# q and k of the later batches transposed by the DMA crossbar instead of TensorE, in a fused window-attention and MLP kernel

## Chip, cores and metric

The kernel runs on one core of a Trainium2 chip. The metric is the device time of one execution in microseconds. Before the change it is 324.88 us (median of two runs, 324.31 to 325.46).

## The reference

```python
# q, k, v: (8 batches, 8 heads, 576 tokens, 64), fp32
scores = q @ k.T / sqrt(64); masked to the 64 newest tokens (0 <= i - j < 64)
x = softmax(scores) @ v                      # then heads are joined: (8, 576, 512)
xn = (x - mean) / sqrt(var + 1e-6) * g_ln
out = x + relu(xn @ w_ch1) @ w_ch2           # 512 -> 2048 -> 512, fp32
```

One caution. The inputs are small (0.1 times a normal draw), so the softmax is nearly flat. "Correct" is therefore weak evidence that q and k are laid out right.

## The kernel before

There are nine groups. Group g (0 to 7) runs the MLP of the first 512 tokens of batch g; group 8 runs it for the four "tails" (the last 64 tokens of each batch, two batches in one tail). From group 2 on, a group is 30 units of TensorE work: 16 of the first layer (`l1`), 14 of the second. The attention of later batches is slotted between these units by `at(unit, function, ...)`. Each engine runs its instructions in this program order.

```python
def load_qk(b, half):                        # b >= 2: 4 tokens (1 KB) in one run
    ...
    nc.sync.dma_start(out=t[:, :].rearrange("p (h m) -> p h m", h=4),
        in_=src[b, 4*half:4*half+4, 0:SM, :].rearrange("h (p j) d -> p h (j d)", j=4))

def t_main(b, x, half, eng=None):            # TensorE transposes, then an eviction
    src = qk16.pop((b, x, half))
    tp = t_tile([128, 8, 128], f"tp_{b}_{x}_{half}")
    for i in range(8):
        nc.tensor.transpose(out=tp[:, i, :], in_=src[:, i], identity=ident16)
    ...
    evac(...)                                # ScalarE in the later batches

def t_tail(i, x): ...                        # the same for a tail: 4 (q) or 8 (k) transposes

# the schedule, groups g > 1; b = g + 1, n = g + 2 (cut)
TAILS = {3: [0], 5: [1], 7: [2, 3]}          # group: tails whose attention runs in it
at((2, 7, 12, 17)[j], b_step, b, j)          # values into xps (one PSUM tile), normalise into x_norm
at(1, s_mm, NGRP-1, i)                       # scores of a tail, slot 1 of its group
at(11, cast_qk, n, 0); at(16, cast_qk, n, 1) # GpSimd, fp32 -> fp16
at(17, t_main, n, 0, 0); ...                 # slots 17, 19, 21, 25
at(17, load_qk, n+1, 0); at(18, load_qk, n+1, 1); at(23, load_v, n+1, 0, 4)
at(27, s_mm, n, 0)                           # first scores of batch n
at(24, cast_tail, i); at(27, t_tail, i, 0); at(29, t_tail, i, 1)  # group before the tail's
# units 27 and 29 store two blocks each: nc.sync.dma_start(out=out[...], in_=x_norm...)
```

The loads of q, k, v and the weights and all stores but one at the very end are issued by SyncE and share one in-order queue.

The softmax here doesn't subtract the row's maximum and nothing guards it: scores larger than these inputs give would overflow.

## Time and profile before

| | before |
|---|---|
| time, median | 324.88 us |
| span of the profiled execution | 322.6 us |
| TensorE busy, share of the chain of waits | 96%, 85% |
| mean granted TensorE clock | 0.996 |
| one steady group (2 to 6) | about 33 us |

From the page of the kernel before, the slices: one digit for each fortieth of the span, in tenths; `PEclk` is the granted TensorE clock, `DMA` the mean busy share of the DMA engines. Below it, the chain that ended last, by engine.

```profile
PE   7978999999989999999999999999999999999993
...
PEclk9999999999999999999999999999999999999998
DMA  8999999976089947904598459000570190003013
...
PE 85%; DVE 4%; SPq 3%; DMA 2%; POOL 2%; ACT 1%; issue 0%; ACTq 0%; POOLq 0%
```

The PE row is what bounds the kernel: from the fifth slice on it is nearly always 9. DMA has room on average, but not everywhere.

The chain that ended last, in order of time (start, duration, what), around the end of group 2. These are the transposes that the change removes:

```profile
117.87 0.55 PE tp L216 x8
...
120.39 0.45 PE tp L216 x8
...
131.36 0.45 PE tpk L237 x8
```

Eight transposes lengthen the chain by 0.45 us (the first eight of a group by 0.55). The busy column of the grouped view says more (some 220 ns each), because matmuls overlap.

The same stretch by windows of 2 us (window, length, then busy us and instructions of PE, weight loads, DVE, ACT and POOL, the clock, the DMA share and GB/s):

```profile
116.00:118.00 2.00, 2.00 (x34) 1.62 (x33) 1.97 (x5) 0.38 (x1) 1.80 (x4) 1.00 0.99 347
...
126.00:128.00 2.00, 2.00 (x24) 1.84 (x23) 1.11 (x2) 0.77 (x1) 2.00 (x5) 1.00 0.92 223
...
132.00:134.00 2.00, 2.00 (x25) 0.89 (x23) 0.09 (x1) 1.78 (x3) 0.00 (x0) 1.00 1.28 254
```

At 116 us the DMA engines are full with 1 KB q and k runs, at 347 GB/s; at 126 us they are nearly full with 256-byte v runs, at 223 GB/s; at 132 us they are still full, with stores. (The share, as the profile counts it, can exceed 1.) Two lines of the timeline show who will need the queue's output next (start, duration, engine, line, instruction, and in brackets the idle time before it and what ended it):

```profile
133.47 0.41 PE L263 MATMUL sc<-tqT,tkT 64*128 64x64 f16 x16
...
135.66 0.69 DVE L297 TENSOR_TENSOR xn<-xps,rcp 128x512 f32<-128x512 f32 x1 [0.19 <-DMA out_dram<-xn]
```

A tail's scores start 1.7 us into group 3, and VectorE already waits 0.19 us for the last store of group 2, whose buffer it overwrites.

### The profile page before, as it was taken

The page shows a single profiled execution, that of the slowest core. Times are in us where ns is not written, and L with a number is a line of the kernel's source. Part 1 is how long each engine was busy: PE and PEld are TensorE (multiplying, and loading weights), DVE is VectorE, ACT ScalarE, POOL GpSimd, SP SyncE. Part 2 cuts the span into 40 slices and gives each one's busy share as a digit, 9 for nine tenths or more (in the row PEclk, how much of TensorE's full clock was granted, in tenths as well). Part 3 has the DMA queues.
Part 4 walks back from the last instruction along what each step waited for, and adds up shares of the span by engine and source line. Part 5 has one row for each costly group of instructions (what it writes and reads, how often), then busy time and mean ns, then how long its engine had stood idle before and what let it go on. Part 6 is the DMA issues. An engine that isn't in the chain of part 4 may idle for free.

```text
span 322.6 us, 7813 instructions
## 1 busy us (share of the span) xinstructions
PE 309.6 (96%) x3229; PEld 204.6 (63%) x3229; DVE 204.3 (63%) x388; ACT 176.8 (55%) x292; POOL 164.6 (51%) x251
## 2 busy tenths in 40 slices
PE   7978999999989999999999999999999999999993
PEld 4556444687544578656964696459755865694582
DVE  0887764666885795489447954896559644751643
ACT  2576624487346754876457647775486157405600
POOL 7678765423991689079705982598036506200000
PEclk9999999999999999999999999999999999999998
DMA  8999999976089947904598459000570190003013
GB/s 194 282 385 259 363 306 295 264 267 133 35 276 227 207 139 204 241 2 133 173 259 183 132 168 259 26 2 2 171 182 2 24 241 33 0 2 131 0 36 98
DMA packets 85639, 51.08 MB, mean 158 GB/s; under 512 B 55682, under 2 KB 76674, under 8 KB 85603
## 3 DMA queue, kind: packets, MB, share of 16 engines
q1 hardware_dynamic: 84816, 48.11, 55.6%
q0 software_dynamic: 640, 2.33, 3.1%
q8 instruction: 25, 0.41, 0.5%
q10 hardware_dynamic: 146, 0.13, 0.1%
q14 instruction: 12, 0.09, 0.1%
HBM read 38.80 MB, written 9.44 MB: 150 GB/s over the span
## 4 chain that ended last, share of the span: by engine, by line
PE 85%; DVE 4%; SPq 3%; DMA 2%; POOL 2%; ACT 1%; issue 0%; ACTq 0%; POOLq 0%
PE hps L363 33%; PE pA L435 11%; PE pC L435 8%; PE pB L435 8%; PE hph L484 6%; PE ch L375 4%; PE xps L291 4%; PE tp L216 3%; PE sc L263 3%; DMA w1s<-in_moe_w_ch_dram 2%; PE ztp L328 2%; SPq L139 2%; POOL w1g L188 1%; PE ch L499 1%; DVE wT L532 1%; SPq L87 1%
## 5 line engine op out<-in xcount | busy, mean ns | idle before, releaser
L363 PE MATMUL hps<-zT,w1g 128*128 128x512 f16 x480 | 112.0, 379 | 0.0
L367 ACT ACTIVATE hrT<-hps 128x512 f16<-128x512 f32 x120 | 71.9, 599 | 35.1 <-PE hps L363 31.6
L363 PEld LDWEIGHTS <-w1g 128*128 128x128 f16 x480 | 44.1, 98 | 47.0 <-issue 1.0
L316 POOL TENSOR_SCALAR rsz<-mvg 128x1 f32<-128x1 f32 x28 | 12.2, 437 | 76.5 <-DVE mvg L302 75.5
L266 ACT ACTIVATE pt<-sc 128x512 f16<-128x512 f32 x72 | 39.0, 595 | 14.6 <-PE sc L263 13.1
L435 PEld LDWEIGHTS <-sS 128*128 128x128 f16 x448 | 43.0, 98 | 4.7
L207 ACT COPY qkT<-tp 128x1024 f16<-128x1024 f16 x26 | 26.2, 1012 | 33.6 <-PE tp L216 32.4
L126 POOL CAST qk<-qk 128x1024 f16<-128x1024 f32 x32 | 33.7, 1070 | 9.5 <-DMA qk<-in_q_dram 4.9
L442 DVE TENSOR_TENSOR xn<-pA,xn 128x512 f32<-128x512 f32 x28 | 19.2, 686 | 26.1 <-PE pA L435 17.4
L331 ACT COPY zT<-ztp 128x512 f16<-128x512 f16 x36 | 21.1, 586 | 26.5 <-PE ztp L328 26.1
L435 PEld LDWEIGHTS <-hrT 128*128 128x128 f16 x336 | 32.3, 98 | 5.0
L294 DVE RECIPROCAL rcp<-xps 128x8 f32<-128x8 f32 x36 | 7.4, 205 | 34.3 <-PE xps L291 34.1
L414 DVE TENSOR_TENSOR sS<-hrT 128x512 f16<-128x512 f16 (+1 forms) x42 | 21.4, 510 | 10.2 <-ACT hrT L367 10.2
L297 DVE TENSOR_TENSOR xn<-xps,rcp 128x512 f32<-128x512 f32 x36 | 24.9, 692 | 3.3 <-DMA out_dram<-xn 2.2
L435 PE MATMUL pA<-wT,sS 128*128 128x256 f16 x224 | 26.9, 273 | 0.0
L435 PE MATMUL pC<-w2s,sS 128*128 128x256 f16 x224 | 26.8, 273 | 0.0
L273 DVE TENSOR_TENSOR pt<-pt,mask 128x1024 f16<-128x1024 f16 x28 | 21.2, 762 | 8.6 <-ACT pt L266 8.5
L484 PE MATMUL hph<-zT,w1g 128*128 128x256 f16 x192 | 23.6, 273 | 2.5 <-ACT zT L331 1.1
L299 DVE BATCH_NORM_STATS2 stats<-xn 128x6 f32<-128x512 f32 x36 | 25.0, 695 | 1.2
L319 POOL TENSOR_SCALAR z<-xn,rsz 128x512 f16<-128x512 f32 x28 | 23.4, 836 | 2.9
L375 PE MATMUL ch<-w2s,hrT 128*128 128x512 f16 x96 | 23.7, 380 | 0.1
L484 PEld LDWEIGHTS <-w1g 128*128 128x128 f16 x192 | 18.0, 98 | 5.8 <-issue 2.2
(85 smaller groups left out, 437.2 us busy)
## 6 DMA issues: line engine op xcount, KB each, us to landing
out_dram<-xn SPq DMA_DIRECT2D x34, 256.0 KB, 3.6
qk<-in_q_dram SPq DMA_DIRECT2D x16, 512.0 KB, 4.8
qk<-in_k_dram SPq DMA_DIRECT2D x16, 512.0 KB, 5.9
v<-in_v_dram SPq DMA_DIRECT2D x32, 256.0 KB, 6.2
w2s<-in_moe_w_ch_dram SPq DMA_DIRECT2D x12, 512.0 KB, 5.6
w1s<-in_moe_w_ch_dram SPq DMA_DIRECT2D x4, 512.0 KB, 7.3
tk<-in_k_dram SPq DMA_DIRECT2D x8, 256.0 KB, 4.4
tv<-in_v_dram SPq DMA_DIRECT2D x8, 256.0 KB, 5.1
```

The lines of the kernel that those rows point to most:

```text
L126: nc.gpsimd.tensor_copy(out=dst[:, :].rearrange("p (a j) e d -> p a e j d", j=j), in_=t[:, :].rearrange("p (a e j d) -> p a e j d", e=2, j ...
L207: nc.scalar.copy(out=out, in_=in_)
L266: nc.scalar.activation(out=pt[:, par], in_=sc[par], func=AF.Exp, bias=0.0, scale=scale)
L297: nc.vector.tensor_tensor(out=xn, in0=xps[:, :, 0:D], in1=rcp_b, op=ALU.mult)
L299: nc.vector.bn_stats(out=stats, in_=xv)
L319: nc.gpsimd.tensor_scalar(out=z, in0=xv, scalar1=rs, scalar2=nm, op0=ALU.mult, op1=ALU.add)
L363: nc.tensor.matmul(out=hps, lhsT=w1g[:, kc, 128 * hc:128 * (hc + 1)], rhs=zT[g][:, kc, :], start=(kc == 0), stop=(kc == NKC - 1),)
L367: nc.scalar.activation(out=hrT[:, hc, :], in_=hps, func=AF.Relu, bias=0.0, scale=1.0)
L375: nc.tensor.matmul(out=ch[kb], lhsT=hrT[:, hc, 128 * kb:128 * (kb + 1)], rhs=w2s[:, hc, :], start=(hc == 0), stop=(hc == NHC - 1),)
L414: nc.vector.tensor_tensor(out=o, in0=x, in1=y, op=op)
L435: nc.tensor.matmul(out=bank[which][:, p, :], lhsT=a[:, c, 128 * p:128 * p + 128], rhs=wv[:, c, :], start=(first and p == 0 and c == 0), st ...
L484: nc.tensor.matmul(out=hps[:, e], lhsT=w1g[:, kc, 128 * hc:128 * (hc + 1)], rhs=zT[g][:, kc, 256 * half:256 * half + 256], start=(kc == 0) ...
```

## The change

The intent: take 176 transposes off the engine that bounds the kernel. q and k of batches 4 to 7 are loaded with a token on each partition, cast into one fp16 tile per tensor, and transposed by the DMA crossbar, one instruction for q and one for k of a batch; the tails likewise.

```diff
+    XQ = 4
+    cast16 = [p_const.tile([128, NHP, 4, 128], FP16, ...) for x in range(2)]
 def load_qk(b, half):
+            elif b >= XQ:
+                for c in range(2):
+                    s0 = 256 * half + 128 * c
+                    nc.sync.dma_start(out=t[:, 512*c:512*c+512]...,
+                        in_=src[b, :, s0:s0 + 128, :].rearrange("h s d -> s h d"))
 def t_main(b, x, half, eng=None):
+        if b >= XQ:
+            if half == 0:
+                dst = flat(b, x)[:, 64 * x:64 * x + NHP * SM]
+                nc.sync.dma_start_transpose(out=dst.rearrange("p (a t) -> p a t", t=128),
+                                            in_=cast16[x][...].rearrange("p a c m -> p (a c m)"))
+            return
 def t_tail(i, x):
+            if XQ < B:
+                nc.sync.dma_start_transpose(out=tailT[i][x]..., in_=src...)
+                return
 # schedule
-            for ... in zip((17, 19, 21, 25), ((0, 0), (1, 0), (0, 1), (1, 1))):
+            for ... in zip((17, 17, 17, 17) if n >= XQ else (17, 19, 21, 25), ...):
                 at(i, t_main, n, x, half, 0)
```

(Cut: the casts into `cast16`, the score matmuls' addressing of the flat layout, fewer zero fills, and a switch `XZ = 99` that leaves another use of the crossbar off.) A k tail is cast into `cast16[1]` too. No load or store moved in the program, but two transposes now stand ahead of the next batch's loads in SyncE's queue.

More of the change, by code (lines that the diff above doesn't have):

```diff
@@ L41 @@
     EPS = 1e-6
+    XQ = 4
+    XZ = 99
     scale = 1.0 / (D ** 0.5)
@@ L77 @@
     qk32, qk16, v32 = {}, {}, {}
+    cast16 = [p_const.tile([128, NHP, 4, 128], FP16, tag=f"cast16_{x}", name=f"cast16_{x}") for x in range(2)]
     tail32, tail16, tailT, vT = {}, {}, {}, {}
@@ L90, in load_qk @@
                 )
+            elif b >= XQ:
+                for c in range(2):
+                    s0 = 256 * half + 128 * c
+                    nc.sync.dma_start(
+                        out=t[:, 512 * c:512 * c + 512].rearrange("p (h d) -> p h d", h=H),
+                        in_=src[b, :, s0:s0 + 128, :].rearrange("h s d -> s h d"),
+                    )
             else:
@@ L110, in cast_tail @@
         q16 = p_in.tile([128, H, D], FP16, tag="tq16", name=f"tq16_{i}", bufs=1)
-        k16 = p_in.tile([128, 2, H, D], FP16, tag="qk16_1", name=f"tk16_{i}")
+        k16 = cast16[1][:, 0:2].rearrange("p r c (e d) -> p r (c e) d", d=D)
         vt = p_va.tile([128, 2, H, D + 1], FP16, tag="vt", name=f"vt_{i}", bufs=1)
@@ L122, in cast_qk @@
             t = qk32.pop((b, x, half))
-            dst = p_in.tile([128, 8, 2, D], FP16, tag=f"qk16_{x}", name=f"qk16_{x}_{b}_{half}")
+            if b >= XQ:
+                nc.gpsimd.tensor_copy(
+                    out=cast16[x][:, :, 2 * half:2 * half + 2, :].rearrange("p a c m -> p c a m"),
+                    in_=t[:, :].rearrange("p (c a m) -> p c a m", c=2, a=NHP),
+                )
+                continue
+            dst = cast16[x][:, 2 * half:2 * half + 2, :, :].rearrange("p a c (e d) -> p (a c) e d", d=D)
             qk16[(b, x, half)] = dst
@@ L202, in alloc_qkT, with flat @@
         qkT[b] = [p_qkt.tile([128, NHP, SM + 64 * x], FP16, tag=f"qkT{x}", name=f"qkT{x}_{b}") for x in range(2)]
-        nc.gpsimd.memset(qkT[b][1][:, :, 0:64], 0.0)
+        if b < XQ:
+            nc.gpsimd.memset(qkT[b][1][:, :, 0:64], 0.0)
+        else:
+            nc.gpsimd.memset(qkT[b][1][:, 0, 0:64], 0.0)
+    def flat(b, x):
+        return qkT[b][x][:, :, :].rearrange("p h m -> p (h m)")
     def evac(x, out, in_):
@@ L211, in t_main @@
     def t_main(b, x, half, eng=None):
+        if b >= XQ:
+            if half == 0:
+                dst = flat(b, x)[:, 64 * x:64 * x + NHP * SM]
+                nc.sync.dma_start_transpose(out=dst.rearrange("p (a t) -> p a t", t=128),
+                                            in_=cast16[x][:, :, :, :].rearrange("p a c m -> p (a c m)"))
+            return
         src = qk16.pop((b, x, half))
@@ L229, in t_tail @@
                         p_qkt.tile([128, 2, NHP, 128], FP16, tag="tkT", name=f"tkT_{i}", bufs=1))
+            if XQ < B:
+                nc.sync.dma_start_transpose(out=tailT[i][0], in_=src[:, :, :].rearrange("p h d -> p (h d)"))
+                return
             tp = t_tile([128, NHP, 128], f"tpq_{i}")
@@ L233, in t_tail @@
         else:
+            if XQ < B:
+                nc.sync.dma_start_transpose(out=tailT[i][1][:, :, :, :].rearrange("p r h t -> p (r h) t"),
+                                            in_=src[:, :, :, :].rearrange("p r h d -> p (r h d)"))
+                return
             tp = t_tile([128, 2, NHP, 128], f"tpk_{i}")
@@ L258, in s_mm @@
                         rhs = tailT[j][0][rows, hp, 64 * iw:64 * iw + 64]
+                    elif g >= XQ:
+                        c0 = SM * hp + 64 * (2 * j + iw)
+                        lhsT = flat(g, 1)[rows, c0:c0 + 128]
+                        rhs = flat(g, 0)[rows, c0:c0 + 64]
                     else:
@@ L325, in zt_step @@
             zT[g] = p_grp.tile([128, NKC, 512], FP16, tag="zT" + sfx, name=f"zT_{g}", bufs=1 if sfx else 2)
+        if g >= XZ:
+            nc.sync.dma_start_transpose(out=zT[g][:, :, 128 * kb:128 * kb + 128], in_=z)
+            return
         ztp = t_tile([128, NKC, 128], f"ztp_{g}_{kb}")
@@ L745 @@
             at(21, make_vB, n)
-            for i, (x, half) in zip((17, 19, 21, 25), ((0, 0), (1, 0), (0, 1), (1, 1))):
+            for i, (x, half) in zip((17, 17, 17, 17) if n >= XQ else (17, 19, 21, 25),
+                                    ((0, 0), (1, 0), (0, 1), (1, 1))):
                 at(i, t_main, n, x, half, 0)
```

## The prediction

> **What bounds it now.** TensorE. The page's busy table has PE at 96% of the 322.6 us span and the chain of waits gives it 85%; in the steady groups (33 us each, from 99 us) the timeline shows it back to back at full clock. The DMA engines, by stretches of 2 us, are at 0.9 to 1.28 from 126 to 136 us, the end of group 2, when v loads, vB copies and 1 MB of stores overlap; the same in group 4. Their last stores land so late that VectorE's normalise at 135.66 already waits for one (0.19 us; 1.67 us at 170).
>
> **What goes.** Sixteen 8-transpose blocks of batches 4 to 7 (0.45 us of the chain each), four k-tail blocks (0.45) and four q-tail blocks (about 0.22): 7.2 + 1.8 + 0.9 = 9.9 us of TensorE, all on the critical path. ScalarE loses 20 evacuations of 1012 ns and 4 of 588, off the path.
>
> **What comes.** All on SyncE's one in-order queue:
> - q and k loads of these batches in 256-byte runs instead of 1 KB. The old ones ran at 347 GB/s (share 0.99), 256-byte v loads at 223 GB/s (share 0.92). So 2 MB per batch takes about 8.7 us instead of 6.
> - Transposes of 4 + 1.5 MB in all. The Trainium skill, "DMA: Bandwidth & Descriptors", section "Latency and other measured facts", states 261 GB/s for a DMA transpose; no run here shows it yet. Estimate from it: 2 us per 512 KB.
> - Order. The q/k transposes wait for both casts (about 119 to 120 us in group 2), and the next batch's q/k loads (at 114 us before) stand behind them. Then come v, two stores, the q-tail transpose, two stores, and last the k-tail transpose.
>
> **Where it bites (estimates).** From 119 us the queue has 4 us of transposes, 8.7 of q/k, about 10 of v, copies and stores, and 1.5 of tail transposes: the k-tail tile lands near 145 us. The tail's score matmuls want it in slot 1 of the next group (at 133.5 us before, about 131 after the savings), in TensorE's order. So:
> - groups 3 and 5 (tail, after a group with loads): about 14 us of stall each;
> - group 4: its first normalise waits for late stores, and TensorE for the xps bank: about 6 us;
> - group 7: tail, no q/k loads before it: about 4.5 us;
> - first scores of batches 4 to 7: about 1.5 us in all.
>
> Sum: 324.9 - 9.9 + 28 + 6 + 4.5 + 1.5 = 355 us, less a little overlap.
>
> **Predicted: 352 us, 8 in 10 between 327 and 380.** Faster by over 2%: 0.07. Within 2%: 0.07. Slower by over 2%: 0.86.
>
> **What would show each step right.** No TensorE transposes of tq, tk and batches 4 to 7; ScalarE down 22 us. In the list of waits a new, long wait of TensorE for the tail score operands (tkT, released by a DMA), two of more than 8 us; a DVE wait for out_dram of several us at group 4's start. DMA share near 1 from about 120 us to 145 us. Main transposes landing 2 to 6 us after issue. First scores of batches 4 to 7 waiting over 2 us each would mean slower transposes.
>
> **What would make it wrong.** Transposes and loads overlapping better than a shared DMA budget allows: then most of the 10 us remains as a gain (315 to 318). Transposes far slower than 261 GB/s, for instance limited by SyncE issuing many small pieces: each k-tail wait grows by over 10 us, towards 380 and beyond.

## The result, and the profile after

| | before | after |
|---|---|---|
| time, median | 324.88 us | 375.37 us (375.18 to 375.55, 2 runs) |
| ratio of the fast runs | | 1.155 (1.146 to 1.165) |
| span of the profiled execution | 322.6 us | 373.5 us |
| share of the chain: PE, SyncE's queue, DMA | 85%, 3%, 2% | 49%, 19%, 13% |
| mean granted clock | 0.996 | 0.919 |

Ratios are the mean time of one kernel's fast runs over that of the other's fast runs of the same rounds, so they differ a little from the ratio of the medians.

The kernel became 50.5 us slower. The same rows of the page, after:

```profile
PE   7889999999899911999908990099999985999994
...
PEclk9999999999999975899965996579999996999998
DMA  8999999654996999008996299900785094203013
...
PE 49%; SPq 19%; DMA 13%; DVE 7%; POOL 6%; issue 3%; ACT 0%; POOLq 0%; DVEq 0%; ACTq 0%
```

Two things are new in these rows: holes in PE (1, 1; 0; 0, 0; and a shallow one, 8, 5, in group 7), and a 5 to 8 in the clock row at and behind each hole. Before, the clock row was 9 but for the last slice.

The new waits of TensorE, and the one of VectorE behind one of them, from the list of who waited for whom (total us, times, longest):

```profile
PE sc L302 <- DMA tkT<-cast: 40.7, 4, 17.4
...
DVE xn L336 <- DMA out_dram<-xn: 12.1, 1, 12.1
...
PE xps L330 <- DVE pt L312: 9.8, 1, 9.8
...
PE sc L302 <- DMA qkT<-cast: 0.6, 1, 0.6
```

They are six places, which the timeline of TensorE alone shows with the idle time ahead of each in brackets:

```profile
127.93 0.41 PE L302 MATMUL sc<-qkT,qkT 64*128 64x64 f16 x16 [0.59 <-DMA qkT<-cast]
...
148.21 0.61 PE L302 MATMUL sc<-tqT,tkT 64*128 64x64 f16 x16 [16.30 <-DMA tkT<-cast]
...
197.47 0.26 PE L330 MATMUL xps<-vB,pt 128*64 128x65 f16 x1 [9.83 <-DVE pt L312]
...
242.12 0.61 PE L302 MATMUL sc<-tqT,tkT 64*128 64x64 f16 x16 [17.37 <-DMA tkT<-cast]
...
312.43 0.61 PE L302 MATMUL sc<-tqT,tkT 64*128 64x64 f16 x16 [6.18 <-DMA tkT<-cast]
...
323.92 0.41 PE L302 MATMUL sc<-tqT,tkT 64*128 64x64 f16 x16 [0.89 <-DMA tkT<-cast]
```

(The first line is the only wait for a transposed main tile, 0.59 us; then come the tail in group 3, the `xps` bank in group 4, the tail in group 5 and the two tails in group 7.) The main transposes themselves are in time. What is late is the k tail, and SyncE's queue shows why. This is its timeline from the main transposes of group 2 to the k tail's:

```profile
119.21 4.56 SPq L237 DMA_TRANSPOSE qkT<-cast  x2
123.81 1.77 SPq L97 DMA_DIRECT2D qk<-in_q_dram  x2
125.63 3.21 SPq L97 DMA_DIRECT2D qk<-in_k_dram  x2
128.88 4.57 SPq L97 DMA_DIRECT2D qk<-in_q_dram  x2
133.50 1.87 SPq L97 DMA_DIRECT2D qk<-in_k_dram  x2
135.47 4.99 SPq L155 DMA_DIRECT2D v<-in_v_dram  x4
140.55 1.55 SPq L443 DMA_DIRECT2D out_dram<-xn  x2
142.20 1.37 SPq L259 DMA_TRANSPOSE tqT<-tq  x1
143.66 1.00 SPq L443 DMA_DIRECT2D out_dram<-xn  x2
144.75 1.28 SPq L266 DMA_TRANSPOSE tkT<-cast  x1
```

The same queue before, where the q and k loads of batch 5 went out one by one from 114.06 us on, and v and the stores were issued by 133.4 us:

```profile
114.06 0.37 SPq L92 DMA_DIRECT2D qk<-in_q_dram  x1
...
125.07 4.44 SPq L139 DMA_DIRECT2D v<-in_v_dram  x4
129.70 3.70 SPq L401 DMA_DIRECT2D out_dram<-xn  x4
```

After, these loads are issued from 123.81 us. They take 11.6 us to issue, v takes 5.0, and the k tail's transpose leaves at 144.75 us and lands (its data are complete) 3.4 us later. Its score matmuls were ready at 131.9 us. The windows of this stretch:

```profile
121.00:123.00 2.00, 2.00 (x20) 1.80 (x19) 1.67 (x4) 0.00 (x0) 1.76 (x5) 1.00 1.13 200
...
134.00:136.00 2.00, 0.00 (x0) 0.00 (x0) 0.00 (x0) 0.00 (x0) 0.00 (x0) 0.85 0.91 206
...
140.00:142.00 2.00, 0.00 (x0) 0.00 (x0) 0.00 (x0) 0.00 (x0) 0.00 (x0) 0.50 1.15 210
...
150.00:152.00 2.00, 2.00 (x35) 1.10 (x34) 0.69 (x2) 0.80 (x2) 0.00 (x0) 0.50 0.00 0
...
152.00:154.00 2.00, 2.00 (x9) 0.83 (x8) 1.93 (x5) 1.49 (x4) 0.67 (x2) 0.88 0.01 4
```

The DMA engines are busy nearly throughout (a mean share of 0.79 from 132.0 to 135.4 us and of 1.15 from there to 140.5) while the compute engines stand still. And the clock: it is halved from about 135.4 us (0.85 in the window from 134: 1.4 us at full speed, 0.6 at half), 3.5 us after TensorE fell idle, and it stays at half until about 152.5 us, over 4 us after work was back at 148.21. In the other three long stalls it fell 2.4, 2.8 and 3.2 us after TensorE fell idle.

Group 4 has no tail. There the late stores block VectorE, whose normalise overwrites `x_norm`, and TensorE finds `xps` full:

```profile
195.20 0.69 DVE L336 TENSOR_TENSOR xn<-xps,rcp 128x512 f32<-128x512 f32 x1 [12.08 <-DMA out_dram<-xn]
```

### The profile page after: what moved, and what is told of

Its sections match the earlier page's. It is cut to its first block, busy times and chain, and to the rows that moved or that the text cites. A ratio compares the mean times of both kernels' runs of the same rounds, so it can differ in the third digit from the quotient of the medians.

```text
span 373.5 us, 7489 instructions
## 1 busy us (share of the span) xinstructions
PE 309.2 (83%) x3053; PEld 197.8 (53%) x3053; DVE 200.4 (54%) x388; ACT 156.2 (42%) x268; POOL 162.9 (44%) x251
## 4 chain that ended last, share of the span: by engine, by line
PE 49%; SPq 19%; DMA 13%; DVE 7%; POOL 6%; issue 3%; ACT 0%; POOLq 0%; DVEq 0%; ACTq 0%
PE hps L405 22%; SPq L97 9%; PE pA L477 6%; SPq L155 5%; PE hph L526 4%; PE pB L477 4%; PE pC L477 4%; DMA tkT<-cast 4%; DMA w2s<-in_moe_w_ch_dram 3%; DMA qk<-in_k_dram 3%; PE xps L330 3%; PE ch L417 2%; PE sc L302 2%; SPq L443 2%; DMA w1s<-in_moe_w_ch_dram 2%
## 5 line engine op out<-in xcount | busy, mean ns | idle before, releaser
L405 PE MATMUL hps<-zT,w1g 128*128 128x512 f16 x480 | 118.7, 397 | 0.0
L405 PEld LDWEIGHTS <-w1g 128*128 128x128 f16 x480 | 45.9, 101 | 52.0 <-issue 8.5
L302 PE MATMUL sc<-tqT,tkT 64*128 64x64 f16 x64 | 2.2, 226 | 40.7 <-DMA tkT<-cast 40.7
L312 DVE TENSOR_TENSOR pt<-pt,mask 128x1024 f16<-128x1024 f16 x28 | 20.5, 737 | 13.5 <-ACT pt L305 13.4
L330 PEld LDWEIGHTS <-pt 128*64 128x64 f16 x576 | 12.7, 114 | 24.1 <-DVE pt L312 10.8
L302 PEld LDWEIGHTS <-tkT 64*128 64x128 f16 x64 | 1.6, 116 | 42.7 <-DMA tkT<-cast 42.7
```

The lines of the kernel that those rows point to most:

```text
L330: nc.tensor.matmul(out=xps[64 * r:64 * r + 64, h, :D + 1], lhsT=pt[:, par, hp, r, :], rhs=rhs, start=True, stop=True)
L405: nc.tensor.matmul(out=hps, lhsT=w1g[:, kc, 128 * hc:128 * (hc + 1)], rhs=zT[g][:, kc, :], start=(kc == 0), stop=(kc == NKC - 1),)
```

## The experiments

The theories, by the letters of the expectations. **Q**, mine: queue order; the tail transposes and the stores stand behind the next q, k and v loads, in a queue that the main transposes hold up. **X**: the crossbar transposes are too slow in themselves or disturb what runs beside them. **L**: the 256-byte load runs cost the time. For the clock, **I**: TensorE's idle time lowers it; **T**: something else does (power, the crossbar). All twelve kernels gave a result that passed the comparison. "Before" in each comparison is the kernel before (324.5 to 325.2 us median).

| run | what | median us | ratio to before | mean clock |
|---|---|---|---|---|
| e1_tails_pe | tails back on TensorE | 357.28 | 1.098 | 0.954 |
| e3_layout_only | new loads and layout, no crossbar | 327.90 | 1.009 | 0.999 |
| e4_long_runs | crossbar, old 1 KB runs (scrambled) | 365.18 | 1.125 | 0.935 |
| e7_fill | dummy matmuls in the idle stretches | 372.39 | 1.146 | 0.978 |
| e7b_fill_more | the same, enough of them | 373.27 | 1.150 | 1.000 |
| e5_loads_last | next loads last in the queue | 341.68 | 1.052 | 0.971 |
| e10_tails_dma_only | only the tails on the crossbar | 347.56 | 1.070 | 0.973 |
| e8_reordered | queue by deadlines | 332.61 | 1.025 | 0.987 |
| e11_tails_late | e8, tails in groups 6 and 7 | 340.29 | 1.045 | 0.974 |
| b1_before_tails_late | control: before, tails in 6 and 7 | 328.05 (3 fast runs) | 1.010 | 0.996 to 0.998 (its profile is of the slow run) |
| e12_reorder_tails_pe | reordered, tails on TensorE | 318.15 | 0.978 | 0.998 |
| e13_deadline_order | all on the crossbar, reordered further | 321.64 | 0.990 | 0.998 |

### Tails back on TensorE

```diff
 def t_tail(i, x):
-            if XQ < B:        # both branches
+            if False:
```

> The changed kernel with the tails transposed by TensorE again (batches 4 to 7 stay on the crossbar). Theory Q (queue order: the tail transposes stand behind the next batch's loads): the 40.7 us of waits for tkT vanish, but the stores stay late behind the same loads, so groups 3 and 5 now show the wait for xps that only group 4 shows (9.8 us each, hidden until now by the longer tail wait), with a low clock after it. About 375 - 40.7 + 2.7 (transposes back) + 2 x 9.8, less some clock: 350 to 358 us. Theory X (the crossbar itself is slow and hurts all it touches): the time falls only by the tail's own transposes, a few us, to about 368.

Measured: 357.28 us, within Q's range. The waits for `tkT` are gone, and the other wait that the late stores make came to light in all three groups that follow a group with loads. TensorE's timeline:

```profile
149.05 0.65 PE L330 MATMUL xps<-vt,pt 128*64 128x65 f16 x16 [10.46 <-POOL rsz L355]
...
194.09 0.26 PE L330 MATMUL xps<-vB,pt 128*64 128x65 f16 x1 [9.60 <-DVE pt L312]
...
237.09 0.65 PE L330 MATMUL xps<-vt,pt 128*64 128x65 f16 x16 [10.37 <-POOL rsz L355]
```

(The engine named in the brackets is the last of several that the profile saw; the bank `xps` is freed by VectorE.) So the tail transposes alone are not the cause: without them the same queue stops TensorE for 10 us, a few units later in the same groups. X, which expected about 368 us, does not fit.

### Loads and layout alone

Main transposes and tails on TensorE, from the token-by-partition tile; loads and casts as changed.

```diff
 def t_main(b, x, half, eng=None):         # b >= XQ
-            nc.sync.dma_start_transpose(...)
+            tp = t_tile([128, NHP, 2, 128], ...)
+            for hp in range(NHP):
+                for c in range(2):
+                    nc.tensor.transpose(out=tp[:, hp, c, :], in_=cast16[x][:, hp, 2*half + c, :], ...)
+            evac(..., qkT[b][x][:, :, c0:c0 + 256]..., tp)
 def t_tail(i, x):
-            if XQ < B:
+            if False:
-            for ... in zip((17, 17, 17, 17) if n >= XQ else (17, 19, 21, 25), ...):
+            for ... in zip((17, 19, 21, 25), ...):
```

> The new token-by-partition loads, casts and layout for batches 4 to 7, but every transpose on TensorE and no DMA transpose at all. Theory Q: the loads are not held behind transposes and take only about 2.7 us more DMA time per batch; stores land some 3 us later, which TensorE's slack covers: 325 to 330 us. Rival L (the 256-byte runs are what slows it): most of the 50 us stays, 350 us or more.

Measured: 327.90 us, 0.9% slower than before (0.7 to 1.1%). Twice TensorE waits 1.5 us for the k tail's cast, whose buffer is now shared with the main tile. L falls: the short runs by themselves cost under 4 us.

### Crossbar with the old runs

```diff
 def load_qk(b, half):
-            elif b >= XQ:
+            elif False:       # 1 KB runs; the tokens come out scrambled
```

> The changed kernel with batches 4 to 7 read in the old 1 KB runs, wrong result on purpose (tokens end up scrambled), all else the same. Theory Q: each chain from the main transposes to the tail transposes is 2.7 us shorter (8.7 to 6 us of loads), so three stalls shrink by 2 to 4 us each: 364 to 369 us. Rival L: most of the stalls go, below 345 us.

Measured: 365.18 us. The three tail waits are 12.82, 14.63 and 6.09 us instead of 16.30, 17.37 and 6.18, and the wait in group 4 is 3.31 us instead of 9.83, with one more of 2.28 us there for a copy of v (`vB`). So each chain of q and k loads is some 3 us longer through the short runs, which with the layout-only run means: run length matters only where the queue is already late. That this scrambled kernel passed is the caution given with the reference.

### Order alone

```diff
             if n + 1 < B:
-                at(17, load_qk, n + 1, 0)
-                at(18, load_qk, n + 1, 1)
-                at(23, load_v, n + 1, 0, 4)
+                at(30, load_qk, n + 1, 0)
+                at(30, load_qk, n + 1, 1)
+                at(30, load_v, n + 1, 0, 4)
```

> Order alone: the changed kernel with the next batch's q, k and v loads issued at the end of the group, behind the tail transposes and stores, instead of between the main transposes and the stores. Same work, same bytes. Theory Q: the 16 to 17 us tail waits shrink to 2 to 5 us (the transpose's own landing time of 3.4 us) and the 10 us wait for xps goes: 323 to 334 us. Theory X (the transposes themselves are too slow or disturb other work): still above 350.

Measured: 341.68 us. The same bytes, the same transposes, and 34 us less than the changed kernel. That is the direct evidence for Q. But I had expected 323 to 334 us. What stayed, in TensorE's timeline:

```profile
135.89 0.61 PE L302 MATMUL sc<-tqT,tkT 64*128 64x64 f16 x16 [3.60 <-DMA tkT<-cast]
...
201.22 0.61 PE L302 MATMUL sc<-qkT,qkT 64*128 64x64 f16 x16 [5.88 <-DMA qkT<-cast]
...
209.83 0.41 PE L302 MATMUL sc<-tqT,tkT 64*128 64x64 f16 x16 [3.29 <-DMA tkT<-cast]
...
279.19 0.61 PE L302 MATMUL sc<-tqT,tkT 64*128 64x64 f16 x16 [6.38 <-DMA tkT<-cast]
```

The 3.3 to 3.6 us waits are about the transpose's own landing time (3.1 to 4.0 us in the changed kernel), since its slot is too close to its use. The new one at 201 us is the main transpose of batch 6 in group 4, which now stands behind batch 6's own loads, moved to the end of group 3, and the next tail's loads: the pair of transposes took 10.24 us to issue there and 4.54 us in group 3.

### Only the tails on the crossbar

The layout-only kernel with the tails' DMA transposes back (`if False` to `if XQ < B` in `t_tail`).

> Batches 4 to 7 transposed by TensorE from the new layout (as in the layout-only run), only the tails by the crossbar. Theory Q: the loads start as early as in the kernel before, so the tail transposes have less in front of them, but v, the stores and the late q/k loads still are: tail waits of 6 to 9 us each instead of 16 to 17, no wait for xps in group 4, 345 to 355 us. If the main transposes do not matter to the tail waits: 16 us each, over 360.

Measured: 347.56 us, in the range, but the waits are smaller than expected: 4.59, 4.37, 5.55 and 0.89 us. With no main transposes ahead of the loads, the 16 to 17 us waits become 4.5 us. The remaining loss is not only these 15.4 us: the granted clock is 0.973, and the layout's own 3 us are in it.

### The clock

```diff
+        if g in (3, 4, 5, 7):   # dummy 128x512 matmuls into a spare bank
+            at({4: 7}.get(g, 1), fill, {3: 66, 4: 36, 5: 70, 7: 16}[g])
```

> The changed kernel with dummy matmuls on TensorE in the four long idle stretches (66, 36, 70 and 16 of 128x512), just ahead of the matmuls that wait. The stalls stay. Theory I (the clock is halved because TensorE idled for some us, and comes back only after some us of work): the clock stays near 1.0, and the half-speed work after each stall goes: 10 us less, 363 to 368 us. Rival T (the clock is taken for another reason, such as power or the crossbar): the low clock stays in these places and the time stays at 373 to 378.

Measured: 372.39 us, not the 363 to 368 I expected. The dummies ended 2.4 to 3.4 us too early, and the clock still fell at three of these four shorter gaps, for 3.5 to 7 us (in group 3: 0.86, 0.50 and 0.78 in the windows from 150 to 156 us); at the gap of 2.40 us, in group 5, it stayed at 1.00. The k tail also landed 5.1 us after issue in group 3, 3.4 us without dummies; why, I don't know. So the run settles neither I nor T, and I filled the gaps fully: 84, 56, 86 and 34 dummies.

> The changed kernel with enough dummy matmuls (84, 56, 86 and 34) to leave no idle stretch over about 2 us ahead of the waiting matmuls; the first try left 2.4 to 3.4 us[...]. Theory I (idle time halves the clock): granted clock 0.99 or more in the mean, and the half-speed work goes; if the tiles land no later than before, 363 to 369 us, if the dummies overrun, up to 371. Rival T: mean clock at or below 0.98.

Measured: 373.27 us, above the range, but the clock row is whole:

```profile
PEclk9999999999999999999999999999999999999999
```

The mean clock is 1.000, with the same transposes and more matmuls. That settles I against T. The profiles of all fast runs together, from 95 us on, show where idle time begins to count: the clock fell at each of 23 waits of 3.1 us or more, at three of seven between 2.28 and 2.84 us, and at none of 1.9 us or less. It fell 2.0 to 5.3 us after TensorE went idle, so after a short wait the half-speed stretch can begin when work is already back. And each half-speed stretch lasted close to a multiple of 3.45 us (3.5, 6.9, 10.3, 13.8, 17.2, 20.5).

The time hardly moved because the dummies kept TensorE longer than the waits had: 18.3, 12.3, 18.7 and 7.5 us, 56.8 together, where the waits had been 49.7. Not all of that is overrun: in group 3 the k tail's transpose was itself issued later, at 146.96 us instead of 144.75. The clock's price can be read past them, from the end of each wait to the next fixed event in the queue or on TensorE:

| from the end of the wait | to | after | filled | difference |
|---|---|---|---|---|
| group 3, tail scores | next main transposes issued | 21.11 us | 19.29 us | 1.82 |
| group 4, xps matmuls | next main transposes issued | 14.87 | 12.37 | 2.50 |
| group 5, tail scores | next main transposes issued | 21.93 | 19.30 | 2.63 |
| group 7, first tail scores | last tail's scores | 11.49 | 9.66 | 1.83 |

Together 8.8 us, less the 7.1 us that TensorE was held longer: close to the 2.1 us by which the median fell.

### Orders that meet the deadlines

First, half of the next q and k ahead of the main transposes, the rest at the group's end, the k tail ahead of the last stores, its scores three slots later (two for the second tail of a group).

```diff
             at(11, cast_qk, g + 2, 0)
+            if g + 3 < B:
+                at(11, load_qk, g + 3, 0)
-            ts = (10, 11, 14, 20) if n else (1, 2, 5, 11)
+            ts = (12, 13, 16, 22) if n else (4, 5, 9, 15)
-                at(17, load_qk, n + 1, 0)
-                at(18, load_qk, n + 1, 1)
-                at(23, load_v, n + 1, 0, 4)
+                at(30, load_qk, n + 1, 1)
+                at(30, load_v, n + 1, 0, 4)
-                at(29, t_tail, i, 1)
+                at(27, t_tail, i, 1)
```

> All transposes stay on the crossbar, but the queue is reordered for deadlines: half of the next q/k loads ahead of the main transposes, the rest and v at the group's end, the k-tail transpose ahead of the last stores, and the tails' scores three slots later. Theory Q: no wait over 2 us is left and the 9.9 us of removed TensorE work shows: 314 to 319 us. Theory X or L: above 330.

Measured: 332.61 us, a miss. The waits in groups 3 and 5 are gone; one is left in group 4, and two of 2.5 us in group 7:

```profile
197.34 0.61 PE L302 MATMUL sc<-qkT,qkT 64*128 64x64 f16 x16 [5.67 <-DMA qkT<-cast]
```

In the queue, the main transposes of group 4 came behind v, the second tail's loads and half of the next q and k, and took 8.76 us to issue; the DMA share was 0.89 to 1.34 in the windows of 2 us from 173 to 195 us. To see whether the tail loads are to blame, the tails moved to groups 6 and 7, where no q, k, v loads are left.

```diff
-    TAILS = {3: [0], 5: [1], 7: [2, 3]}
+    TAILS = {6: [0, 1], 7: [2, 3]}
```

> The reordered kernel with the tails moved to groups 6 and 7, two in each (loads, casts and transposes in groups 5 and 6, where no q, k, v loads are left), everything else the same. Theory Q: in the reordered kernel the 5.7 us wait for batch 6's q came from the tail loads standing ahead of the transposes in group 4, so it goes, and with it most of the low clock; the waits of the late tails (2.5 us each) may stay or double in number. 314 to 322 us. If the wait in group 4 is the transposes' own slowness, it stays: 328 to 334.

Measured: 340.29 us, another miss, yet it answers the question: the wait in group 4 fell from 5.67 to 0.38 us (first scores, at 190 us). The time went to the tails, 4.76, 7.70, 2.84 and 2.63 us: with two tails in a group, the second one's loads are issued ahead of the first one's transposes.

> Control: the kernel before with the same move of the tails to groups 6 and 7 and no other change. The tails' work only moves: 322 to 327 us. If the late tails by themselves are worth more than 2%, then a gain of the run beside it is not the crossbar's.

Measured: 328.05 us, 1.0% slower than before (0.7 to 1.4%), a little above the range. One of its four executions, the profiled one, was a slow run of 452.62 us at a clock of 0.661 and is left out (with it the median is 328.42). The move by itself gains nothing.

Last, two kernels with one tail each in groups 3 and 6 and two in group 7. The first leaves the tails on TensorE:

```diff
 # the kernel with the tails back on TensorE, and
-    TAILS = {3: [0], 5: [1], 7: [2, 3]}
+    TAILS = {3: [0], 6: [1], 7: [2, 3]}
+            if g + 3 < B:
+                at(11, load_qk, g + 3, 0)
-                at(17, load_qk, n + 1, 0)
-                at(18, load_qk, n + 1, 1)
-                at(23, load_v, n + 1, 0, 4)
+                at(30, load_qk, n + 1, 1)
+                at(30, load_v, n + 1, 0, 4)
```

> Batches 4 to 7 on the crossbar with the reordered loads (half of the next q/k ahead of the main transposes, the rest and v at the group's end), the tails on TensorE, and one tail moved from group 5 to group 6, so that no tail loads stand in group 4's queue. Theory Q: no wait of TensorE over 1 us is left, and the 7.2 us of main transposes show: 317 to 322 us. If the waits only wander to other places: 326 or more.

Measured: 318.15 us (317.56 to 318.65), ratio 0.978 (0.975 to 0.981): faster than both kernels, though the interval straddles the 2% mark, so a gain of over 2% is not established. The rows of its page:

```profile
PE   6989999999998999999999999999999999999993
...
PEclk9999999999999999999999999999999999999999
```

And from its list of waits, TensorE's only one for the crossbar:

```profile
PE sc L302 <- DMA qkT<-cast: 0.6, 1, 0.6
```

The 6.5 us between the medians (324.69 before) are nearly the 7.2 us of the chain that the main transposes had. That they are the cause is argued and not isolated: the kernel before was not run with the same moves of the loads and of one tail.

The second keeps all transposes on the crossbar: the first reordered kernel with these `TAILS`, the last tail's loads at slot 28, its cast at 6, its transposes at 9 and 10, its scores at 16.

> All transposes on the crossbar: the reordered kernel with one tail moved from group 5 to 6, and the last tail's loads put behind the third tail's transposes in the queue, with its scores four slots later. Theory Q: both sources of the reordered kernel's waits (tail loads ahead of batch 6's transposes, 5.7 us; the last tails, 2.5 us each) are gone, so 314 to 320 us. If the waits only wander: 326 or more.

Measured: 321.64 us, ratio 0.990 (0.987 to 0.994), above the range. Moving the tails' 2.7 us as well made it 3.5 us slower: one k tail is still awaited for 1.87 us, and TensorE now waits 4.8 us (1.4 before) for normalised blocks from GpSimd, two of these waits (1.86 and 0.82 us) at the tails' later slots. In the kernel of 318.15 us that wait is 1.4 us.

## Why the prediction was right, and where it was short

The direction was right, and so was the mechanism: the new loads stand behind the main transposes in SyncE's queue; the k tail is the last to land and stops TensorE in groups 3 and 5; in group 4 the late stores do it through VectorE and the `xps` bank; group 7 is hit less. Moving only the loads (341.68 us), or only taking the main transposes away (347.56 us), shrinks these waits, as it should. The time, 375.37 us, lies in the range of 327 to 380 us, but at its end: I predicted 27 us of loss and it was 50.5. The terms:

| term | predicted us | measured us |
|---|---|---|
| TensorE work removed | -9.9 | not read alone; 7.2 of it gave 6.5 in the 318.15 us kernel |
| tail waits, groups 3 and 5 | 28 | 16.30 + 17.37 = 33.7 |
| wait for xps, group 4 | 6 | 9.8 |
| tail waits, group 7 | 4.5 | 6.18 + 0.89 = 7.1 |
| first scores of batches 4 to 7 | 1.5 | 0.6 |
| half clock behind the waits | none | 8.8 |

With -9.9 the measured terms add up to 50.1 us; the half clock is a term of its own, measured by the filled kernel.

- **The missing term** is the clock. The Trainium skill, "TensorE: Matmul & The Clock Gate", section "Part 1: The HAM clock gate (the "warmup" mystery)", states that an idle window of about 3.4 us halves the clock and a busy one restores it. I predicted four stalls of 4.5 to 14 us and did not put its price on them. This trace agrees in size on the way down (2.4 to 3.5 us after TensorE fell idle) and shows 3.9 to 6.2 us at half speed after work was back. The filled kernel shows that the gaps are the cause.
- **The mis-sized term** is the chain in front of the k tail. I gave the q and k loads 8.7 us from the v loads' rate; their issue took 11.6 us, while the main transposes issued just before were still moving (they landed 4.6 and 6.5 us after issue), and beside the `vB` copies issued from 125.4 us. In the order-alone run, with neither in the way, the same loads took 8.1 to 8.9 us to issue. I gave both tail transposes 1.5 us; from the q tail's 1.4 us of issue to the k tail's landing of 3.4 us they took 4.8. Against that, v, copies and stores took some 7.8 us of the queue and not 10, partly since the copies ran beside the q and k loads: without that lucky error the predicted landing at 145 us, against 148.2, would have been further off. The transposes themselves I took at 261 GB/s (the Trainium skill, "DMA: Bandwidth & Descriptors", section "Latency and other measured facts", which gives it for a non-contiguous middle dimension and about 350 to 400 GB/s for the contiguous case); the window from 121 to 123 us, in which SyncE's queue held nothing but transposes, moved 200 GB/s. A main transpose landed 4.4 to 6.5 us after issue, within my 2 to 6 but for its end.
- **Group 4** waits as long as the stores are late, so the same few us made 9.8 out of 6. The run with 1 KB runs confirms the link: 3.31 us there.
- I wrote that ScalarE would lose some 22 us of work; its busy time fell from 176.8 to 156.2 us. It bought nothing, as expected.

What stays open: the 5.1 us landing in the first filled kernel (and one of 5.0 us in the second), how much of the loss in the kernel with only the tails on the crossbar is clock, and whether transposes issued from another engine's queue would have landed sooner, since the DMA engines themselves were busy for most of the wait. That was not tried.

## What to carry to other kernels

Moving work off the busiest engine pays only if the queue that takes it over can meet the deadlines: list, for every item in an in-order DMA queue, what must land when, and put transposes and stores that someone waits for ahead of loads that nobody needs yet. When an estimate contains a stall of TensorE of more than some 3 us, add the half-speed time behind it, about 2 us per stall here. And try the order before judging the idea: with all transposes on the crossbar this kernel was 15.5% slower or 1.0% faster, with the queue order and the slots of the tails as the difference; with the tails back on TensorE it was 2.2% faster.

## What the Trainium skill lacked or had wrong

- "Advanced Engine Details and Errata", section "X-Bar Transpose (TRN2)", says that transpose DMAs on this chip are as fast as regular ones, 350 to 400 GB/s. Here a stretch of nothing but transposes moved 200 GB/s at a DMA share of 1.13, where ordinary 1 KB loads moved 347.
- No page gives, for this chip by name and in microseconds, the issue time of an SBUF-to-SBUF transpose: a 512 KB one held SyncE's queue for 1.9 to 3.6 us in the changed kernel (median 2.2), and landed 4.4 to 6.5 us after issue; a 256 KB one landed after 3.1 to 4.0 us.
- "DMA: Bandwidth & Descriptors", section "Rules for kernel authors", says that a transpose next to ordinary DMAs needs nothing. That row is about correctness, which no run here contradicts; what it leaves out is time: the loads behind two transposes (and beside the `vB` copies) took 11.6 us to issue, against 8.1 to 8.9 us where neither was in the way.
- "TensorE: Matmul & The Clock Gate", section "Part 1: The HAM clock gate (the "warmup" mystery)", gives about 3.4 us of sustained work to restore the clock; after the four waits here it took 3.9 to 6.2 us. It gives an idle window of about 3.4 us to halve it; here waits of 2.28, 2.63 and 2.65 us were enough, while others of 2.40 to 2.84 us were not. It also says that the window runs free of the kernel, and the half-speed stretches of multiples of 3.45 us fit that.
